# ScalarE order in a fused sliding-window attention and highway kernel: q/k evacuation ahead of the second exponential, and blocks 0 and 1 ordered ahead of the transposes of block 2

## Chip, cores, metric

One core of one Trainium2 chip. The metric is the device time of one execution in microseconds (us), as a median of several executions. Results were compared with the reference.

## The reference

Attention over a window of 128 positions plus 4 sink positions at the start of each sequence, then a highway layer over the 512 features that the 8 heads of 64 give together. Batch 4, sequence 768: 3,072 tokens, 24 blocks of 128, six blocks to a sequence.

```python
keep = is_sink | in_window               # pos < 4, or 0 <= row - col < 128
a = softmax(where(keep, q @ k.T / 8, -1e9))
x = (a @ v) -> [3072, 512]               # heads side by side
H = maximum(x @ w_h, 0)
T = sigmoid(x @ w_t + b_t)
out = T * H + (1 - T) * x
```

## The kernel before

One iteration `i` of the main loop works on several blocks at once: scores and exponentials of block i+1, transposes of q and k of block i+2, attention times v of block i, the highway layer of block i-1. Each function below issues instructions to one engine, and its prefix says which; an engine runs its own in that order.

```python
s_ps  = tile_pool(name="ps_s",  bufs=2, space=PSUM)   # sps: scores, 4 KiB a partition
av_ps = tile_pool(name="ps_av", bufs=1, space=PSUM)   # av: 4 KiB
m_ps  = tile_pool(name="ps_m",  bufs=2, space=PSUM)   # tp, xtp, tps, hps, sk in turn: 2 KiB
# ... cut
def pe_T(n):      # TensorE: q and k of block n transposed into tp (m_ps)
def act_T(n):     # ScalarE: nc.scalar.copy(out=qk, in_=tp)      "the q/k copy"
def pe_S(n, g):   # TensorE: scores sps of half g of the heads, from qk
def act_S(n, g):  # ScalarE: e = exp(sps)                        "first/second exponential"
def dve_mask(n, g)                # VectorE: e *= mask
def pe_A(n):      # TensorE: av = e^T v, and the sinks' part from es
def dve_rec(n); def dve_x(n)      # VectorE: xh = av / sum
def pe_X(n); def act_X(n)         # xh transposed into xtp (m_ps), copied to xT
def pe_Mt(n):     # TensorE: tps = bias + xT w_t   (m_ps)
def act_u(n):     # ScalarE: u = tanh(tps)
def pe_Mh(n):     # TensorE: hps = xT w_h          (m_ps)
def dve_d(n):     # VectorE: dd = max(hps, 0) - xh
def pe_sink(n):   # TensorE: sk, the sinks' scores of two blocks (m_ps)
def act_sink(n):  # ScalarE: es = exp(sk)
# ... cut
for i in range(-2, NB + 2):
    ms, os_ = highway(i), highway(i - 1)      # blocks i-1 and i-2
    # ... cut
    if has_sink(i): act_sink(i)               # i % 6 is 2 or 4
    if on(i + 1):
        pe_S(i + 1, 0); act_S(i + 1, 0); pe_S(i + 1, 1)
    if on(i - 1): pe_X(i - 1); act_X(i - 1)
    for o in os_: dve_d(o)
    if on(i): dve_mask(i, 1)
    if on(i + 1): act_S(i + 1, 1)             # second exponential
    if on(i + 2): pe_T(i + 2)
    for o in os_: dve_e(o)
    if on(i): pe_A(i)
    if on(i + 2): act_T(i + 2)                # the q/k copy
    if on(i + 1): dve_mask(i + 1, 0)
    # ... cut: dve_rec(i), dve_o, dve_x(i)
    for m in ms:
        pe_Mt(m); act_u(m); pe_Mh(m)
    if has_sink(i + 1): pe_sink(i + 1)
    # ... cut: loads of later blocks
```

(The statements are joined on one line here to save room.) The pools fill PSUM: 2 x 4 + 4 + 2 x 2 KiB a partition, which is the 8 banks of 2 KiB that the Trainium skill gives ("PSUM — Partial Sum Buffer", Specifications (TRN2)). So no third buffer can simply be added to `m_ps`. In an iteration without sinks the four users go round: xtp takes buffer A, tp B, tps A, hps B.

The softmax here doesn't subtract the row's maximum and nothing guards it: scores larger than these inputs give would overflow.

## Time and profile before

| | before |
|---|---|
| time, median of 4 | 146.31 us (146.04 to 146.74) |
| span of the profiled execution | 145.0 us |
| six iterations in the steady loop | 30.03 us |
| first exponential of block 3 (iteration 2) | 28.54 us |
| first exponential of block 4 (iteration 3) | 33.45 us |
| first exponential of block 23 (iteration 22) to the end | 16.0 us |

The rows from the third on come from the timeline: the start of a block's first exponential is used as a mark of the iteration.

From the page of the profiled execution, the span and the busy time of each engine:

```profile
span 145.0 us, 3266 instructions
PE 115.4 (80%) x1312; PEld 74.8 (52%) x1312; DVE 96.9 (67%) x214; ACT 98.0 (68%) x129; POOL 73.6 (51%) x98
```

No engine is full, so one has to ask who waits for whom. From the list of waits, longest first (total us, times, longest us):

```profile
DVE dd L342 <- PE hps L336: 26.2, 24, 1.5
...
ACT e L251 <- PE sps L243: 12.7, 16, 0.9
...
PE hps L336 <- ACT qk L203: 9.4, 17, 0.7
...
PE tp L196 <- DMA qsd<-in_q_dram: 6.9, 2, 6.7
```

VectorE has the longest waits, but those end when TensorE finishes hps, and TensorE itself waits for ScalarE's q/k copy. hps does not read q or k; it needs the PSUM buffer that the copy empties. The chain of waits shows the whole circle, here for one iteration (start us, duration us, what):

```profile
48.16 1.11 ACT e L251
49.28 0.48 ACT xT L315
49.75 1.02 ACT e L251
50.77 0.91 ACT qk L203
...
51.72 1.02 PE hps L336 x4
52.75 0.35 PE sps L243 x8
...
53.12 1.11 ACT e L251
```

The stretches of time show the loop (last line) and the startup (columns: stretch, its length, then busy us and instruction count of PE, PEld, DVE, ACT and POOL, the granted clock of TensorE as a share of full speed; the last two columns, DMA share and GB/s, are not used here):

```profile
12.00:18.00 6.00, 0.07 (x2) 0.00 (x0) 0.69 (x1) 1.80 (x2) 4.45 (x6) 0.50 1.41 165
...
24.00:26.00 2.00, 2.00 (x17) 1.45 (x15) 0.69 (x2) 1.47 (x2) 2.00 (x4) 0.50 2.38 158
26.00:28.00 2.00, 2.00 (x16) 1.05 (x14) 0.49 (x2) 0.60 (x1) 2.00 (x3) 0.97 2.47 154
48.10:78.20 30.10, 26.95 (x336) 17.75 (x330) 22.64 (x43) 23.97 (x33) 21.46 (x28) 1.00 1.61 147
```

From 12 to 18 us TensorE does nothing and its clock is at half. The timeline of TensorE shows why (in brackets: idle time before, and what ended it):

```profile
18.77 0.61 PE L196 MATMUL tp<-ident,qsd 128*128 128x128 f16 x4 [6.70 <-DMA qsd<-in_q_dram]
19.60 0.61 PE L198 MATMUL tp<-ident,ksd 128*128 128x128 f16 x4 [0.22 <-DMA ksd<-in_k_dram]
20.00 0.95 PE L277 MATMUL av<-v,e 128*128 128x112 f16 x8
```

The attention of block 0 (`av` at 20.00) stands behind the transposes of block 2, and those wait for a load.

### The profile page before, as it was taken

How to read it: one execution, taken by the hardware profiler on the slowest of the kernel's cores; microseconds unless marked ns; L12 is line 12 of the kernel's file. 1: busy time of each engine (PE TensorE's matmuls, PEld its weight loads, DVE VectorE, ACT ScalarE, POOL GpSimd, SP SyncE). 2: the span in 40 equal slices, each digit the busy share in tenths (PEclk: the TensorE clock that was granted, in tenths of full speed). 3: DMA queues.
4: the chain of work that ended last, by engine and by line, in shares of the span. 5: the costliest groups of instructions: out<-in, count | busy, mean ns of one | idle time of the engine just before them, and what ended most of it. 6: DMA issues, size and time to landing. Idle time of an engine off the chain costs nothing.

```text
span 145.0 us, 3266 instructions
## 1 busy us (share of the span) xinstructions
PE 115.4 (80%) x1312; PEld 74.8 (52%) x1312; DVE 96.9 (67%) x214; ACT 98.0 (68%) x129; POOL 73.6 (51%) x98
## 2 busy tenths in 40 slices
PE   6632069989889988988899789889897988998840
PEld 2122058557646654765666358458464664664410
DVE  7441016578659856966868687678677866968770
ACT  3176029497787877977976797798769778976310
POOL 6999599999969999735099770000300000000000
PEclk9975555899999999999999999999999999999996
DMA  1999999999999999999929999210221021021111
GB/s 10 113 112 168 165 155 158 153 156 197 163 190 195 191 183 150 195 194 152 74 74 147 150 197 161 73 73 3 75 77 72 1 77 72 0 77 72 72 72 72
DMA packets 79728, 17.00 MB, mean 117 GB/s; under 512 B 75617, under 2 KB 76641, under 8 KB 79714
## 3 DMA queue, kind: packets, MB, share of 16 engines
q0 software_dynamic: 76256, 10.51, 107.8%
q1 hardware_dynamic: 3458, 6.30, 12.1%
q8 instruction: 10, 0.16, 0.4%
q14 instruction: 4, 0.03, 0.1%
HBM read 21.01 MB, written 6.29 MB: 188 GB/s over the span
## 4 chain that ended last, share of the span: by engine, by line
ACT 41%; PE 35%; POOL 7%; DMA 5%; issue 5%; DVE 4%; POOLq 0%; DVEq 0%
ACT e L251 25%; PE hps L336 16%; ACT qk L203 11%; DMA ksd<-in_k_dram 5%; PE tps L323 4%; ACT xT L315 4%; PE av L277 4%; PE sps L243 4%; DVE dd L342 3%; PE sk L221 3%; POOL qsd L85 2%; PE tps L321 1%; POOL ksd L86 1%; POOL v L93 1%; PE tp L198 1%
## 5 line engine op out<-in xcount | busy, mean ns | idle before, releaser
L251 ACT ACTIVATE e<-sps,ebias 128x1024 f16<-128x1024 f32 (+1 forms) x48 | 49.8, 1041 | 12.7 <-PE sps L243 12.7
L342 DVE SCALAR_TENSOR_TENSOR dd<-hps,xh 128x512 f16<-128x512 f32 x24 | 16.6, 692 | 26.2 <-PE hps L336 26.2
L262 DVE TENSOR_TENSOR e<-e,mask 128x1024 f16<-128x1024 f16 (+1 forms) x48 | 30.7, 640 | 4.4 <-ACT e L251 4.0
L203 ACT COPY qk<-tp 128x1024 f16<-128x1024 f16 x24 | 24.3, 1015 | 11.7 <-PE tp L198 11.7
L336 PE MATMUL hps<-wh_sb,xT 128*128 128x512 f16 x96 | 24.6, 378 | 9.4 <-ACT qk L203 9.4
L85 POOL DMA_DIRECT2D qsd<-in_q_dram x24 | 22.4, 932 | 7.6 <-PE tp L198 5.0
L323 PE MATMUL tps<-wt_sb,xT 128*128 128x512 f16 x96 | 25.0, 383 | 0.0
L277 PE MATMUL av<-v,e 128*128 128x112 f16 x352 | 24.4, 218 | 0.7 <-DVE e L262 0.7
L86 POOL DMA_DIRECT2D ksd<-in_k_dram x24 | 22.2, 925 | 1.1 <-PE av L283 1.0
L93 POOL DMA_DIRECT2D v<-in_v_dram x24 | 22.5, 937 | 0.0
L277 PEld LDWEIGHTS <-e 128*128 128x128 f16 x352 | 21.3, 101 | 1.1 <-DVE e L262 0.9
L336 PEld LDWEIGHTS <-xT 128*128 128x128 f16 x96 | 9.3, 97 | 23.5 <-issue 14.1
L329 ACT ACTIVATE u<-tps 128x512 f16<-128x512 f32 x24 | 14.7, 613 | 6.9 <-PE tps L323 6.8
L243 PE MATMUL sps<-qk 64*128 64x128 f16 x352 | 14.8, 225 | 2.6 <-ACT qk L203 2.6
L348 DVE SCALAR_TENSOR_TENSOR ee<-u,dd 128x512 f16<-128x512 f16 x24 | 16.5, 686 | 0.2
L296 DVE TENSOR_TENSOR xh<-av,rec 128x512 f16<-128x512 f32 x24 | 16.4, 685 | 0.1
L196 PE MATMUL tp<-ident,qsd 128*128 128x128 f16 x96 | 9.9, 230 | 7.2 <-DMA qsd<-in_q_dram 6.9
L354 DVE SCALAR_TENSOR_TENSOR otok<-xh,ee 128x512 f32<-128x512 f16 x24 | 15.6, 648 | 0.1
L243 PEld LDWEIGHTS <-qk 64*128 64x128 f16 x352 | 10.7, 98 | 9.4 <-issue 7.3
L323 PEld LDWEIGHTS <-xT 128*128 128x128 f16 x96 | 9.5, 99 | 11.0 <-issue 1.8
L315 ACT COPY xT<-xtp 128x512 f16<-128x512 f16 x24 | 13.7, 572 | 1.0 <-PE xtp L310 1.0
L212 POOL COPY ks<-qk 64x16 f16<-64x16 f16 x8 | 1.6, 201 | 21.1 <-ACT qk L203 20.9
(49 smaller groups left out, 103.3 us busy)
## 6 DMA issues: line engine op xcount, KB each, us to landing
out_dram<-otok SPq DMA_DIRECT2D x24, 256.0 KB, 2.2
qsd<-in_q_dram POOLq DMA_DIRECT2D x24, 128.0 KB, 5.7
ksd<-in_k_dram POOLq DMA_DIRECT2D x24, 128.0 KB, 5.7
v<-in_v_dram POOLq DMA_DIRECT2D x24, 128.0 KB, 6.1
wt_sb<-in_moe_w_t_dram POOLq DMA_DIRECT2D x1, 512.0 KB, 6.7
wh_sb<-in_moe_w_h_dram POOLq DMA_DIRECT2D x1, 512.0 KB, 8.8
vd<-in_v_dram POOLq DMA_DIRECT2D x4, 4.0 KB, 4.2
bt<-in_moe_b_t_dram SPq DMA_DIRECT2D x1, 2.0 KB
```

The lines of the kernel that those rows point to most:

```text
L85: nc.gpsimd.dma_start(out=qsd, in_=q[b, :, rows, :].transpose([1, 0, 2]))
L86: nc.gpsimd.dma_start(out=ksd, in_=k[b, :, rows, :].transpose([1, 0, 2]))
L93: nc.gpsimd.dma_start(out=vt[:, :, 0:D], in_=v[b, :, rows, :].transpose([1, 0, 2]))
L203: nc.scalar.copy(out=qk, in_=tp_of.pop(n))
L243: nc.tensor.matmul(sps[:, hh, o:o + P], lhsT=kk[rows, hp, :], rhs=qT[rows, hp, :], start=True, stop=True)
L251: nc.scalar.activation(out=e.rearrange("p a b c d -> p a (b c d)"), in_=sps[:, :, 0:2 * np_ * P], func=AF.Exp, bias=ebias, scale=SCALE)
L262: nc.vector.tensor_tensor(out=ev, in0=ev, in1=m.unsqueeze(1).to_broadcast([P, 4, np_ * P]), op=ALU.mult)
L277: nc.tensor.matmul(av[:, g, 2 * hl + hh, 0:_AVN], lhsT=e[:, hh, hl, pc, :], rhs=vt[:, 65 * h:65 * h + _AVN], start=first, stop=False, skip ...
L315: nc.scalar.copy(out=xT, in_=xtp_of.pop(n))
L323: nc.tensor.matmul(tps, lhsT=xT[:, kc, :], rhs=wt_sb[:, kc, :], start=False, stop=(kc == NOC - 1))
L336: nc.tensor.matmul(hps, lhsT=xT[:, kc, :], rhs=wh_sb[:, kc, :], start=(kc == 0), stop=(kc == NOC - 1))
L342: nc.vector.scalar_tensor_tensor(out=dd, in0=h_of.pop(n), scalar=0.0, in1=xh_of[n], op0=ALU.max, op1=ALU.subtract)
```

## The change

Two intents. In the loop, ScalarE copies q and k out of PSUM before the second exponential, so that the buffer comes free earlier. In the startup, attention of blocks 0 and 1 and the highway layer of block 0 are issued ahead of the transposes of block 2, to fill the wait for its load. The arithmetic is unchanged.

```diff
--- before.py
+++ after.py
@@ -375,7 +375,7 @@
                 more_constants()
             if has_sink(i):
                 act_sink(i)
-            if on(i + 1):
+            if i >= 2 and on(i + 1):
                 pe_S(i + 1, 0)
                 act_S(i + 1, 0)
                 pe_S(i + 1, 1)
@@ -383,20 +383,20 @@
                 pe_X(i - 1)
                 act_X(i - 1)
             for o in os_:
-                dve_d(o)
+                if o not in dd_of:
+                    dve_d(o)
             if on(i):
                 dve_mask(i, 1)
-            if on(i + 1):
+            if i >= 2 and on(i + 2):
+                pe_T(i + 2)
+                act_T(i + 2)
+            if i >= 2 and on(i + 1):
                 act_S(i + 1, 1)
-            if on(i + 2):
-                pe_T(i + 2)
             for o in os_:
                 dve_e(o)
             if on(i):
                 pe_A(i)
-            if on(i + 2):
-                act_T(i + 2)
-            if on(i + 1):
+            if i >= 2 and on(i + 1):
                 dve_mask(i + 1, 0)
             if on(i):
                 dve_rec(i)
@@ -410,6 +410,20 @@
                 pe_Mt(m)
                 act_u(m)
                 pe_Mh(m)
+            if i == 1:
+                dve_d(0)
+                pe_T(2)
+                act_T(2)
+            if -1 <= i < 2:
+                for g in range(2):
+                    pe_S(i + 1, g)
+                    act_S(i + 1, g)
+                dve_mask(i + 1, 0)
+            if i < 2:
+                n = {-2: 0, -1: 1, 1: 3}.get(i)
+                if n is not None:
+                    pe_T(n)
+                    act_T(n)
             if has_sink(i + 1):
                 pe_sink(i + 1)
             if i == 0:
@@ -422,7 +436,7 @@
                     sink_v(b, nc.gpsimd)
                 if b + 1 < B:
                     load_sink_v(b + 1)
-            for n in (range(3, AHEAD + 1) if i == -2 else [i + 2 + AHEAD]):
+            for n in {-2: range(3, AHEAD + 1), 0: [], 1: [10, 11]}.get(i, [i + 2 + AHEAD]):
                 if n < NB:
                     if n > 3:
                         load_qk(n)
```

From iteration 2 on, TensorE's and VectorE's orders are those of before (but for the dd of block 0, which has moved ahead); only ScalarE's differs.

## The prediction

> **What bounds the kernel now.** From 28.5 to 129 us it is a loop of 20 block iterations, 5.02 us each (30.03 us per six; timeline, starts of each block's first exponential). No engine is full: in 48.1 to 78.2 us PE is busy 26.95 of 30.1 us, ScalarE 23.97, VectorE 22.64 (busy times of stretches). The chain of waits shows a latency loop of ScalarE and PE: first exponential 1.11, xT copy 0.47, second exponential 1.02, q/k copy 0.91, highway matmul hps 1.02, score matmuls 0.35: 4.9 us. hps waits for the q/k copy (list of waits: 9.4 us in 17 waits, up to 0.7): two buffers of PSUM are shared, and hps takes the one that tp leaves. VectorE then waits for hps (26.2 us in 24), ScalarE for the scores (12.7 in 16).
>
> In the startup PE waits 6.7 us for block 2's q (18.77 us) and then k (19.60), although attention of block 0, queued behind these transposes, could run. The Trainium skill ("TensorE: Matmul & The Clock Gate", Part 2) says that only weight loads are pulled ahead and matmuls stay in program order; the trace agrees: av of block 0 runs at 20.0 us.
>
> **What the change does.** No work is added or removed.
>
> (a) Loop: the q/k copy moves before the second exponential and ends 1.02 us earlier. hps then follows tps without its 0.7 us wait. The new loop should be hps, dd (0.75), transposes tp (0.60), av with sinks (1.02), tps (1.08), hps (0.86): 4.35 us. Solving the order by hand with the trace's durations gives 4.0 us where av is half size, 4.35 usually, and 4.9 where sink-score matmuls (0.46) end the iteration, as these wait up to 0.4 us for tanh, now last on ScalarE. That is 26.9 us per six against 30.03: 10.4 us over the 20 iterations, all on the critical path.
>
> (b) Startup: attention of 0 and 1 and the highway of 0 fill the wait. Behind block 2's arrival stay its copy 1.0, scores, two exponentials 2.1, block 3's copy 1.0, sink scores. The scores of block 3, at 28.06 us before, come at 25.3 to 26.5 us. From this goes what clock is lost: the granted clock is 0.5 from 12 to 26 us before, and dense PE work at 21 to 26 us lifted it; that stretch now gets gaps. The same page (Part 1) says that the clock is released after some 3.4 us of sustained activity; the trace fits. Released only at 29 to 31 us, 1 to 2 us are lost again. I take 1.5 us of gain (0.3 to 2.8).
>
> The tail from 129 us is unchanged.
>
> **Prediction.** 146.3 - 10.4 - 1.5 = 134.4; with some slips between three engines now each near full, 134.8 us, range 131.5 to 139.0. Faster by over 2%: 0.96; within 2%: 0.03; slower by over 2%: 0.01.
>
> **What would show it.** (a) the wait of hps for the q/k copy gone; six blocks in 26.5 to 27.5 us; VectorE's waits for hps under half; the chain mostly PE with dd; PE over 93% busy mid-kernel. (b) av of block 0 at about 10.5 us, tps of block 0 before 18 us, hps waiting for the weights' DMA until about 18 us; scores of block 3 at 25.3 to 26.5 us; the granted clock at 20 to 30 us.
>
> **What would make it wrong.** A two-buffer PSUM wait that I mis-ordered (tanh or dd holding a buffer at each block) would leave 4.6 to 4.8 us per block: 139 to 142. Late highway weights holding up block 2's transposes, or a cold clock past 31 us, would cost the startup's gain. Loads falling behind would show as transposes waiting for DMA.

## The result

| | before | after |
|---|---|---|
| time, median of 4 | 146.31 us (146.04 to 146.74) | 135.83 us (135.3 to 137.14) |
| span of the profiled execution | 145.0 us | 134.5 us |
| six iterations, three times in a row | 30.03, 30.03, 30.02 us | 27.32, 27.12, 27.12 us |
| first exponential of block 3 | 28.54 us | 26.17 us |
| first exponential of block 4 | 33.45 us | 31.79 us |
| first exponential of block 23 to the end | 16.0 us | 16.1 us |

In the row of six iterations the marks are the first exponentials of blocks 5, 11, 17 and 23. The outputs are right. The ratio is 0.9295 (95% interval 0.9222 to 0.9368). Ratios here are the mean time of one kernel's fast runs over that of the other's of the same rounds, so not quite the ratio of the medians. A kernel's run counts as slow when it is over 1.5% above its fastest.

Between the profiled executions 10.5 us went. Up to the first exponential of block 4 it is 1.66 us; the 19 iterations from there to block 23 give 8.88; the tail gives nothing.

The page after: TensorE does the same work, in 86% instead of 80% of the span.

```profile
span 134.5 us, 3265 instructions
PE 115.6 (86%) x1312; PEld 75.1 (56%) x1312; DVE 97.9 (73%) x214; ACT 98.5 (73%) x129; POOL 73.3 (55%) x98
```

The list of waits after. That of hps for the q/k copy is gone; hps waits only once, for its weights. A small new one is there, of the sinks' scores for tanh:

```profile
DVE dd L342 <- PE hps L336: 14.6, 23, 2.6
...
ACT e L251 <- PE sps L243: 5.7, 14, 0.7
...
PE sk L221 <- ACT u L329: 0.9, 3, 0.3
...
PE hps L336 <- DMA wh_sb<-in_moe_w_h_dram: 0.3, 1, 0.3
```

The chain of waits after, from one iteration that ends with sinks (up to sk) into one that does not:

```profile
60.59 1.02 ACT qk L203
61.62 1.02 ACT e L251
62.63 0.49 ACT u L329
...
63.17 0.61 PE sk L221 x8
63.78 0.55 PE sps L243 x16
...
66.34 0.86 PE tps L323 x4
67.20 0.88 PE hps L336 x4
...
68.11 0.70 DVE dd L342
...
68.85 0.38 PE tp L196 x4
```

It is several chains by turns. In three of the four iterations without sinks at their end it runs down TensorE's own order, with `dd` on VectorE once in a while. In the fourth, number 0 modulo six, the chain of the same trace goes through ScalarE as well: first exponential at 72.80 us, xT copy at 73.91, then tps, hps and scores. In the two of six that end with sinks it runs through ScalarE's whole list and leaves it by tanh (`u`), because `sk` takes the buffer that tanh reads.

The timeline of TensorE in the startup, after:

```profile
9.95 0.95 PE L277 MATMUL av<-v,e 128*128 128x112 f16 x8
...
18.47 1.11 PE L336 MATMUL hps<-wh_sb,xT 128*128 128x512 f16 x4 [0.27 <-DMA wh_sb<-in_moe_w_h_dram]
19.42 0.39 PE L196 MATMUL tp<-ident,qsd 128*128 128x128 f16 x4
20.20 0.40 PE L198 MATMUL tp<-ident,ksd 128*128 128x128 f16 x4 [0.39 <-DMA ksd<-in_k_dram]
...
25.20 0.38 PE L221 MATMUL sk<-qk,ks 128*128 128x128 f16 x4 [1.83 <-ACT qk L203]
```

The early work fits into the wait. But TensorE now idles after block 2's arrival, up to the wait of 1.83 us for block 3's q/k copy, and in the stretches after the clock (the column before the last two) falls back to half; e7 below tests that the gap is the cause. The last line shows how full TensorE is in the loop (26.09 of 27.00 us):

```profile
22.00:24.00 2.00, 1.27 (x24) 0.87 (x19) 0.69 (x1) 1.87 (x2) 2.00 (x4) 1.00 2.42 150
24.00:26.00 2.00, 0.80 (x14) 0.69 (x15) 1.29 (x2) 1.53 (x3) 2.00 (x3) 0.87 2.43 155
26.00:28.00 2.00, 2.00 (x27) 1.80 (x22) 0.69 (x1) 1.70 (x4) 2.00 (x3) 0.50 2.43 155
28.00:30.00 2.00, 2.00 (x22) 1.56 (x20) 0.49 (x3) 2.00 (x2) 2.00 (x4) 0.77 2.42 154
44.00:71.00 27.00, 26.09 (x327) 17.50 (x325) 23.05 (x42) 23.96 (x32) 23.16 (x31) 1.00 2.05 181
```

Iteration 2 runs at half clock: 5.62 us between its mark and the next (26.17 to 31.79), where before took 4.91.

### The profile page after: what moved, and what is told of

Same layout as the page of the kernel before. It is cut to its first block, busy times and chain, and to the rows that moved or that the text cites. A ratio compares the mean times of both kernels' runs of the same rounds, so it can differ in the third digit from the quotient of the medians.

```text
span 134.5 us, 3265 instructions
## 1 busy us (share of the span) xinstructions
PE 115.6 (86%) x1312; PEld 75.1 (56%) x1312; DVE 97.9 (73%) x214; ACT 98.5 (73%) x129; POOL 73.3 (55%) x98
## 4 chain that ended last, share of the span: by engine, by line
PE 49%; ACT 24%; POOL 7%; DVE 6%; DMA 6%; issue 4%; POOLq 0%; DVEq 0%
ACT e L251 13%; PE hps L336 10%; PE tps L323 10%; PE av L277 8%; ACT qk L203 7%; PE sps L243 6%; DMA ksd<-in_k_dram 6%; DVE dd L342 4%; PE sk L221 3%; PE tps L321 3%; ACT u L329 3%; PE tp L196 2%; PE tp L198 2%; PE xtp L310 2%; POOL qsd L85 2%
## 5 line engine op out<-in xcount | busy, mean ns | idle before, releaser
L262 DVE TENSOR_TENSOR e<-e,mask 128x1024 f16<-128x1024 f16 (+1 forms) x48 | 31.6, 659 | 9.8 <-ACT e L251 9.8
L277 PE MATMUL av<-v,e 128*128 128x112 f16 x352 | 25.3, 221 | 2.4 <-DVE e L262 2.4
L342 DVE SCALAR_TENSOR_TENSOR dd<-hps,xh 128x512 f16<-128x512 f32 x24 | 16.6, 692 | 14.6 <-PE hps L336 14.6
L323 PE MATMUL tps<-wt_sb,xT 128*128 128x512 f16 x96 | 25.5, 390 | 0.0
L198 PE MATMUL tp<-ident,ksd 128*128 128x128 f16 x96 | 9.8, 227 | 1.3 <-DMA ksd<-in_k_dram 1.2
```

Of the source, the lines that this page charges most:

```text
L262: nc.vector.tensor_tensor(out=ev, in0=ev, in1=m.unsqueeze(1).to_broadcast([P, 4, np_ * P]), op=ALU.mult)
L277: nc.tensor.matmul(av[:, g, 2 * hl + hh, 0:_AVN], lhsT=e[:, hh, hl, pc, :], rhs=vt[:, 65 * h:65 * h + _AVN], start=first, stop=False, skip ...
L323: nc.tensor.matmul(tps, lhsT=xT[:, kc, :], rhs=wt_sb[:, kc, :], start=False, stop=(kc == NOC - 1))
L342: nc.vector.scalar_tensor_tensor(out=dd, in0=h_of.pop(n), scalar=0.0, in1=xh_of[n], op0=ALU.max, op1=ALU.subtract)
```

## The experiments

Two theories about the gain. Mine: the loop gained because the buffer that hps needs is freed one exponential earlier, and this is nearly all; the startup adds one or two us, less what the clock takes. The rival: the early attention of blocks 0 and 1 is what matters, or the scores wait for the q/k copy as data, and the order at the buffer is beside the point. Then comes the question what binds after the change. The table gives all runs. The intervals, in us, are those between the first exponentials of successive blocks in the middle of the loop, by iteration number modulo six (2, 3, 4, 5, 0, 1); those of 3 and 1 end with the sinks' scores. "As" means within 0.02 us; a second stretch of six in the same trace can differ by 0.01.

| kernel | median us | ratio to before | intervals 2, 3, 4, 5, 0, 1 | six |
|---|---|---|---|---|
| before | 146.31 | 1 | 4.92, 5.44, 4.81, 4.46, 4.96, 5.44 | 30.03 |
| change (first runs) | 135.83 | 0.9295 | 4.25, 5.08, 4.14, 4.47, 4.11, 5.07 | 27.12 |
| change (a0, again) | 136.06 | 0.925 | as above | 27.13 |
| e1 loop part alone | 136.31 | 0.9305 | as above | 27.13 |
| e2 startup part alone | 145.03 | 0.9917 | as before | 30.03 |
| e3 before, products swapped | 151.88 | 1.0389 | 5.28, 5.68, 5.27, 4.48, 5.32, 5.68 | 31.71 |
| e4 change, products swapped | 135.6 | 0.9277 | 4.41, 4.90, 4.41, 4.26, 4.32, 4.77 | 27.07 |
| e5 change, sk in av's tile | 134.17 | 0.9182 | 4.26, 4.83, 4.14, 4.47, 4.12, 4.61 | 26.43 |
| e6 e4 and e5 | 133.93 | 0.9164 | 4.38, 4.68, 4.38, 4.25, 4.32, 4.68 | 26.69 |
| e7 change, gap filled | 134.63 | 0.9178 | as the change | 27.13 |
| e8 e5 and e7 | 132.2 | 0.9039 | 4.26, 4.84, 4.14, 4.47, 4.11, 4.61 | 26.43 |
| e9 before without bias (wrong) | 145.78 | 0.996 | 4.92, 5.44, 4.80, 4.25, 4.95, 5.44 | 29.80 |
| e10 change without bias (wrong) | 133.15 | 0.911 | 4.04, 5.07, 3.93, 4.25, 3.95, 5.07 | 26.31 |
| e11 before, sk in av's tile | 146.67 | 1.0021 | as before | 30.03 |

The first runs of before and change stand apart. a0, e1, e2 and e7 ran on one chip (before there: 146.56 median); e3 to e6 on another (146.17); e8 to e11 on a third (146.26). a0 has two slow ones of six; they are left out of its ratio, but not of its median: its four fast runs have a median of 135.72 and a mean of 135.50 us. One of the eleven runs of before beside it is slow too.

### a0_after, e1_loop_only, e2_start_only: the parts

a0 is the change unedited.

> The change itself once more, as the partner of the other runs on this chip. Expected 135 to 136.5 us, ratio 0.93 to the kernel before. Its startup should again show the granted clock falling to 0.5 at about 25 to 29 us, if that is a property of the order and not of one execution.

e1 is the kernel before with this alone:

```diff
-            if on(i + 1):
+            if i < 2 and on(i + 1):
                 act_S(i + 1, 1)
             if on(i + 2):
                 pe_T(i + 2)
+            if i >= 2 and on(i + 2):
+                act_T(i + 2)
+            if i >= 2 and on(i + 1):
+                act_S(i + 1, 1)
 # ...
-            if on(i + 2):
+            if i < 2 and on(i + 2):
                 act_T(i + 2)
```

> The startup of the kernel before, and from iteration 2 on the q/k copy ahead of the second exponential on ScalarE; TensorE's queue is not changed at all. Theory (the loop's gain comes from the PSUM buffer that hps gets earlier, the startup adds its own part): 20 iterations times 0.47 us, so 136.5 to 137.5 us; the wait of hps for the q/k copy is gone; six iterations take 27.1 us. Rival (the earlier attention of blocks 0 and 1 is what matters, the swap alone only moves a wait): 143 us or more.

e2 is the change with the old order in the loop:

```diff
+            if i >= 2 and on(i + 1):
+                act_S(i + 1, 1)
             if i >= 2 and on(i + 2):
                 pe_T(i + 2)
                 act_T(i + 2)
-            if i >= 2 and on(i + 1):
-                act_S(i + 1, 1)
```

> The new startup with the old order of ScalarE in the loop. Theory: only the startup's gain, 1 to 2 us, so 144.3 to 145.3 us, six iterations again 30.0 us. Rival (the startup is worth the 2.4 us by which the exponential of block 3 came earlier): 143.9 us. Together with e1 it shows whether the two parts add up to the 10.5 us measured.

Measured: a0 136.06 us (134.39 to 137.25 in six runs), e1 136.31 (a little under the range said), e2 145.03. In e1 TensorE's and VectorE's queues are instruction for instruction those of before; only two ScalarE instructions change places in each iteration, and 9.8 us of span go (145.0 to 135.2). Six iterations take 27.13 us, and hps no longer waits for the q/k copy. The rival's 143 us is refuted. The startup alone brings 1.5 us by the medians, 1.2 by the means of the fast runs, and 0.6 us by the traces' marks at block 23 (128.97 before, 128.37 in e2). That is less than its rival's 2.4 us: in e2 the exponential of block 3 did come 2.18 us earlier (26.36), but the clock stood at half until after 30 us, and iteration 2 took 6.50 us where before took 4.91. The marks add up: 9.77 in e1 (128.97 to 119.20) and 0.60 in e2, against 10.54 in the change. Given the loop, the startup is worth 0.8 us: a0's mark at block 23 is at 118.43, e1's at 119.20, and the means of the fast runs (135.50 and 136.30) say the same.

a0's profile repeats the half clock in iteration 2 (0.65 from 26 to 28 us, 0.50 from 28 to 30), and 5.90 us for that iteration. e1, whose TensorE is busy without a gap from 22 us on, has 0.99 to 1.00 from 26 us, and 4.26 us.

### e3_before_swap: is it the buffer?

The kernel before; from iteration 2 hps is computed first, then tps, so that tps is the one to take tp's buffer (reads of xT adapted).

```diff
-                pe_Mt(m)
-                act_u(m)
-                pe_Mh(m)
+                pe_Mh(m)
+                pe_Mt(m)
+                act_u(m)
```

> The kernel before, with the two highway products swapped on TensorE from iteration 2 on (hps first, then tps). Now tps gets the PSUM buffer that tp leaves. Theory (a PSUM buffer held until the q/k copy is done is what binds): the wait moves to tps, which waits for the q/k copy and then runs 1.08 us where hps ran 0.86; a loop of 5.15 to 5.25 us, so 149 to 151 us. Rival (the next scores wait for the q/k copy because they need its data): the order of the two products does not matter, 146 to 147 us.

Measured: 151.88 us, ratio 1.0389 (1.0319 to 1.046), somewhat beyond the 149 to 151 expected; the usual interval is 5.28 us where 5.15 to 5.25 was said. The list of waits of this kernel:

```profile
PE tps L321 <- ACT qk L203: 13.9, 17, 0.9
```

The wait stays with the buffer, not with the product: now tps has it, in 17 waits as hps had. If the scores had waited for the copied q and k as data, the swap of two products between would have cost nothing. The size has two parts that can be read from the traces. In an iteration of number 0 modulo six, e3 took 1.77 us from the start of the waiting product to the next exponential (84.31 to 86.08), where before took 1.40 (51.72 to 53.12): tps takes 1.26 us where hps took 1.02, and by e3's chain tanh follows it with 0.49 us ahead of the exponential, where the scores took 0.35. The expectation had left this second part out. So the place of the wait shows the buffer, and the size of the loss is not the buffer's alone. This and e1 show the mechanism.

### e7_warm: what the startup loses to the clock

The change, with nine dummy matmuls of 512 columns of zeros after block 3's transposes in iteration 1, where TensorE waits for the q/k copy. They write the tile of av, which is idle there.

```diff
+            if i == 1:
+                warm_av(9)        # matmuls of zeros into a tile of av_ps, never read
             if has_sink(i + 1):
                 pe_sink(i + 1)
```

> The change with nine dummy matmuls of 512 columns on TensorE in the gap at 23 to 25 us, while it waits for block 3's q/k copy; they write the idle PSUM tile of av. Theory (iteration 2 took 5.6 us instead of 4.9 as the clock was back at half rate from 25.7 to 29 us): the granted clock stays at 1.0 from 20 us on, iteration 2 takes 4.8 to 5.0 us, and the time falls by 0.5 to 0.9 us against the change run beside it. Rival (iteration 2 is long as VectorE and the loads are late there): no change of over 0.2 us.

Measured: 134.63 us (133.64 to 134.98). Against the fast runs of a0 beside it that is 1.0 us by the means (134.51 and 135.50) and 1.1 by the medians; by the marks at block 23 of the two traces it is 1.34 (117.09 and 118.43). The intervals of the two ratios overlap (0.9132 to 0.9225, and 0.9194 to 0.9307), so the reading rests on the traces. The stretches:

```profile
24.00:26.00 2.00, 2.00 (x19) 1.18 (x19) 1.63 (x3) 1.53 (x3) 2.00 (x3) 1.00 2.36 150
26.00:28.00 2.00, 2.00 (x45) 1.88 (x42) 0.52 (x1) 2.00 (x4) 2.00 (x4) 1.00 2.39 152
28.00:30.00 2.00, 2.00 (x14) 0.91 (x11) 1.54 (x4) 2.00 (x3) 2.00 (x3) 1.00 2.36 151
```

The clock stays at 1.00 and iteration 2 takes 4.25 us. The gain is at or above the upper end of the 0.5 to 0.9 us that I expected, and by the marks it is above: I had set the undisturbed iteration at the 4.8 to 5.0 us of the old loop, though the new loop's is 4.25. The rival (loads or VectorE late) fell, since neither was touched. So the early attention does its work, and with the gap filled the startup is worth 2.1 us over e1 (marks at block 4: 32.74 in e1, 31.81 in a0, 30.61 in e7).

### e9_before_nobias, e10_after_nobias: who has slack?

In both kernels the matmul that adds the bias to tps is left out, 0.22 us of TensorE per block. Their outputs are wrong, which doesn't matter for the times.

```diff
-        nc.tensor.matmul(tps, lhsT=ones_row, rhs=bt16, start=True, stop=False)
 # ... first of the four others gets start=True
```

> Wrong result on purpose: the kernel before without the matmul that adds the bias in tps, 0.22 us of TensorE in each block. Theory (the loop of before is bound by the chain through ScalarE, and TensorE has slack while hps waits for the q/k copy): six iterations shrink by at most 0.3 us from 30.0, and with the tail, where tps is on the chain, the whole by 0.5 to 1.6 us. Rival (TensorE's work bounds it already): 24 times 0.22, 5 us.

> Wrong result on purpose: the same matmul left out of the change. Theory (now TensorE's own sequence is the loop in five of six iterations): six iterations shrink by about 0.9 to 1.1 us from 27.1, the whole by 3 to 4.7 us against the change, to 131 to 133 us. Rival (ScalarE or a wait between the engines still sets the pace): under 1.6 us, as in the kernel before.

Measured: before falls by 0.5 us (146.26 to 145.78, ratio 0.996, interval 0.9917 to 1.0003, so hardly clear of noise), with 0.21 us gone from one interval of six and 0.00 or 0.01 from the others. The change falls from 27.12 to 26.31 us per six, 0.81, and in time by about 2 to 2.7 us (ratio 0.911, against 0.925 and 0.9295 of other rounds). I expected 3 to 4.7 us and five of six intervals; it is four. Those of 2, 4, 5 and 0 lose 0.16 to 0.22 us each, those of 3 and 1, which end with the sinks, lose 0.01 at most. So before, TensorE had slack in five intervals of six; after, its tps is on the chain in four, and something else sets the other two.

### e5_sk_av, e11_before_sk_av: the two other intervals

The sinks' scores are written into a tile of av's pool, which is idle when they run, instead of m_ps.

```diff
-        sk = m_ps.tile([P, 2, P], FP32, tag="m", name="sk")
+        sk = av_ps.tile([P, 2, 4, P], FP32, tag="av", name="sk")[:, 0, 0:2, :]
```

> The change, with the sinks' scores sk written into the PSUM tile of av, so that they take no buffer that tanh still reads. Theory (in the two iterations of six that end with sk, sk waits 0.2 to 0.5 us for tanh): these take 4.6 to 4.8 us instead of 5.07, six take 26.3 to 26.5 us, about 133.3 us in all. Rival (TensorE is full there, the wait is only the profile's naming): no change.

> The kernel before with the sinks' scores in the tile of av, as in e5. Theory (the wait of sk for tanh exists only since the change, which put tanh last on ScalarE behind the second exponential): no gain, within 0.4 us of the kernel before, six iterations 30.0 us. Rival (the sinks always waited for a buffer): 1.5 to 2.5 us faster, as in e5.

Measured: in the change the two intervals fall from 5.08 and 5.07 to 4.83 and 4.61 us, the other four stay within 0.01, and six take 26.43 us, as expected. The list after had named only three waits of sk for tanh, 0.9 us over the whole run, while 0.70 us per six is over 2 us in the three sixes measured; the list undervalues them. The chain after is the better guide here: from 44 us on it leaves ScalarE by tanh for sk in every iteration that ends with sinks. The edit also changes who takes which buffer after sk, but in the loop (44 to 118 us) that list has no TensorE wait for a PSUM buffer other than this one. The whole is 134.17 us, ratio 0.9182, a smaller gain than the 133.3 us expected. Its runs fall into two pairs, 133.3 to 133.4 and 134.9 to 135.2 us; the profiled one, of the slower pair, had a long cold start (iteration 2 took 6.32 us), and the others have no trace. In the kernel before the same edit does nothing (1.0021, interval 0.9972 to 1.0071; six in 30.03). So the wait of sk for tanh is made by the change. The reason, read from the traces, is not that tanh became last on ScalarE, as the expectation says: it was last before, too. But before, tanh (0.63 us, from 56.50) ran while hps, which had waited for the same q/k copy, was at work (1.02 us, from 56.68), and sk, behind hps at 57.54, found its buffer free. Now hps no longer waits (it starts at 62.07), tanh still comes behind the second exponential (62.50), and sk has to wait for it until 63.17.

### e4_swap, e6_both: is dd the last link off TensorE?

e4 is the change with hps before tps (the edit of e3), so that dd could run under tps. e6 is e4 with the edit of e5.

> The change, with hps ahead of tps from iteration 2 on. Theory (after the change the loop is hps, dd, tp, av, tps, hps, with dd the only link off TensorE): dd now runs under tps, so most iterations take about 4.2 us instead of 4.35, and the sinks' matmuls wait for dd instead of tanh; six take 26.1 to 26.6 us instead of 27.1, about 133 us. Rival (TensorE is full): no change, 135.5 us; or ScalarE, with tanh now late, becomes the bound: 137 us or more.

> Both e4 and e5. Theory: no link off TensorE is left in the loop, six iterations take 25.3 to 25.8 us (TensorE's own work) and the whole 130 to 131.5 us, the fastest of all. Rival (ScalarE or VectorE is by then the bound): no better than the better one of e4 and e5.

Measured: 27.07 us per six in e4 and 26.69 in e6, where 26.1 to 26.6 and 25.3 to 25.8 were expected. The whole was 135.6 and 133.93 us where about 133 and 130 to 131.5 were expected. My theory of dd failed as a way to gain. The swap shortens the intervals of 5 (4.47 to 4.26) and those with sinks, but lengthens those of 2, 4 and 0. The chain of waits of e4 shows the first reason, at the end of an iteration with sinks:

```profile
60.34 0.69 DVE e L262
...
61.17 0.65 DVE otok L354
61.82 0.60 DVE xh L296
62.42 0.61 DVE dd L342
...
63.07 0.61 PE sk L221 x8
```

`dd` stands behind `otok` and `xh` in VectorE's order, so it starts long after hps is done, and sk waits for the buffer. The chain of e6 shows the second:

```profile
72.13 0.47 issue
72.60 1.11 ACT e L251
73.71 0.49 ACT xT L315
...
74.24 1.04 PE hps L336 x4
```

The chain comes from tps to a tanh on ScalarE, whose start lies just ahead of the 0.47 us called issue, and goes on to exponential, xT and hps: a new circle through ScalarE, in an interval of 4.32 us. With e5 already in, the swap loses (26.43 to 26.69); by the loop the rival of e6 was right. The times do not separate the two (ratios 0.9164 and 0.9182, with intervals of 0.007 either way). How much of the change's loop dd holds stays open.

### e8_sk_av_warm: both edits that gained

> The change with the two edits that gained, the sinks' scores in the tile of av (e5) and the dummy matmuls in the gap of the startup (e7). Theory (two separate losses, one in two iterations of six, one in the startup): the gains add, six iterations take 26.4 us, iteration 2 about 4.3 us, in all 131.8 to 133.0 us. Rival (both free the same time): no better than 133.6 us.

Measured: 132.2 us (132.03 to 132.72 in six runs), ratio 0.9039 (0.9007 to 0.907), correct: the fastest of all (the change had 0.925 and 0.9295), with 26.43 us per six and 4.25 us for iteration 2. The gains add. The runs also spread less, 0.7 us over six against 1.8 us over the four fast ones of a0, on another chip. That the spread of the change comes from the clock in the startup would be a guess; no trace shows it run by run.

## Why the prediction was right

The time, 134.8 us with 131.5 to 139.0, holds the measured 135.83. Point by point:

- **Bound before, and the mechanism in the loop:** right. The circle e, xT, e, q/k copy, hps, scores was the loop; e1 gets 9.8 of 10.5 us by changing ScalarE's order alone, e3 moves the wait to the other product, e9 shows TensorE's slack. This, the larger part of the gain, was no luck.
- **Size of the loop's gain:** 10.4 us was a little too much; the loop part alone, e1, gained 9.77. The loop took 27.12 us per six instead of 26.9, and 27.32 in its first six. The 4.9 us for iterations with sinks measured 5.07 and 5.08, the 4.0 measured 4.11; both are waits I had put a little too short. In the change itself 8.17 us went from the first exponential of block 3 to that of block 23, but this has in it the half clock of iteration 2 (5.62 us against 4.91 before and 4.26 in e1), which the prediction had charged to the startup.
- **The new loop:** half right. TensorE's order with dd was to be the loop. It is the chain in three of six iterations; in a fourth, which e10 also shortens, the chain goes through the first exponential and the xT copy. The two with sinks are ScalarE's list up to tanh (e5), and I had given that wait 0.4 us, on top of a TensorE loop, when it is what sets those iterations.
- **Startup:** its course was right; its size, 1.5 us, was too large. Attention of block 0 at 9.95 us (10.5 said), hps of block 0 at 18.47 waiting for its weights ("about 18"), scores of block 3 at 25.52 (25.3 to 26.5), the clock back at half and released only at about 29 us. By the first exponential of block 4, 1.66 us had gone, but 0.71 of this is the loop's (e1: 33.45 to 32.74). By the marks the startup's own part is 0.6 us alone (e2; 1.2 by the means of the fast runs) and 0.8 given the loop, inside the range of 0.3 to 2.8. e7 gives the price of the clock, 1.0 to 1.34 us ("1 to 2 us").
- **Signs in the profile:** the wait for the q/k copy is gone; six iterations in 27.1 to 27.3 us (26.5 to 27.5 said); TensorE 97% busy in the loop (over 93%). VectorE's waits for hps fell to 14.6 of 26.2 us, not under half. The chain is TensorE 49% and ScalarE 24%, so ScalarE keeps more of it than said.
- **Tail:** unchanged, 16.0 and 16.1 us.
- **The sum:** 10.4 and 1.5 make 11.9 us; 10.5 were measured. By the marks both terms were too large, by 0.6 and 0.7 us, and the allowance of 0.4 us for slips took back a part.

## What to carry to other kernels

A wait for an instruction whose data is not needed is a wait for its buffer: follow the buffer's turn, and put the instruction that frees it ahead of one nobody waits for yet. After such a move the next holder of that pool is the place to look (here tanh, then worth 0.7 us of 27), and a tile elsewhere that is idle at that moment can serve. Work moved forward into a load's wait leaves a gap behind it, and on TensorE that gap had a price in clock here, which a few dummy matmuls bought back.

## What the Trainium skill lacked or had wrong

- "TensorE: Matmul & The Clock Gate", Part 1, gives, among other causes, idle windows of about 3.4 us as what throttles the clock. In the change it fell to half at about 25.5 us though TensorE had been busy 0.70 us of the two from 20 us, 1.27 of the next two and 0.80 of the two after, with no idle gap over 1.83 us from 20.2 us on. The page puts no number on how much work within a window is too little; e7, at 0.52, 1.83 and 2.00 us in the same stretches, kept the full clock. Three groups of matmuls in that stretch of the change are transposes (about 0.4 us each); no run tests whether they count like other work.
- The same page says that the window runs free and that the ramp differs from run to run. This agrees: of two executions of the change, one had 0.50 to 0.55 from 8 to 18 us and the other 1.00. It puts the ramp at under 1% of a typical kernel's span. Here the second loss of clock alone, which e7 undid, was worth 1.0 to 1.34 of 136 us, 0.7 to 1.0%; what the ramp at the start costs on top was not measured.
- The same page, Part 1, calls ScalarE and VectorE strict first in, first out. This agrees, and is the lever: e1 exchanged two ScalarE instructions per iteration and took 9.8 us of span. I found no page that follows how the turn order of a PSUM pool can bind two unrelated products across engines (e3: the wait moved from hps, 17 waits and 9.4 us, to tps, 17 waits and 13.9 us).
